# Segment copies ordered by token group: a linear-attention and expert-layer kernel on one core

## The chip, the cores and the metric

The kernel runs on one NeuronCore of one Trainium2 chip. The metric is the time of one execution on the device in microseconds. The core has five engines that run side by side: TensorE (PE in the rows; PEld is its weight load), VectorE (DVE), ScalarE (ACT), GpSimd (POOL) and SyncE (SP). Each has a sequencer that reads its instructions in order, and engines meet through semaphores. DMA transfers are issued from SP's and POOL's queues.

## What is computed

First a linear attention over q, k and v of shape (8, 8, 576, 64), then a layer of eight experts in which a hash of the token's id chooses the one expert of each token:

```python
q_s = exp(q - max(q)) / sum(...)          # over the head dimension
k_s = exp(k - max(k)) / sum(...)          # over the sequence
kv  = einsum('bhsd,bhse->bhde', k_s, v)
x   = einsum('bhsd,bhde->bhse', q_s, kv)  # regrouped as (4608, 512)
expert_idx = token_ids * 2654435761 % 8
for e in range(8):
    xe = x[expert_idx == e]
    out[expert_idx == e] = relu(xe @ w1[e]) @ w2[e]   # w1: 512 x 1024, w2: 1024 x 512
```

## The kernel before

The program is written engine by engine: every operation is appended to its engine's list in the order of the Python code, and `Emit._waits` adds the semaphore waits that its reads (R), writes (W) and partial writes (P) need. A write waits for an earlier write to the same buffer even on the same engine; only TensorE is excepted. Nothing reorders the lists.

**First stage, eight batches.** For batch b the loop of line 734 loads q, k and v (lines 493 to 497, from SP's queue), takes exponentials on ACT (lines 500 and 504, tiles eq and ek), transposes q on TensorE (line 514; the copies to qT are lines 524 to 529), casts v on DVE (line 509), forms kv (line 537) and its normalised form kvn (line 546), the row sums (lines 556 and 560), and attends (lines 564 and 569), which leaves the batch's tokens in xn. One batch later `sort` (lines 584 to 596) multiplies xn by one-hot matrices, so that the tokens of each of two groups (384 and 192 tokens) stand in order of expert, and ACT copies the result from PSUM to xs (line 595). There are two xs buffers, used in turn.

**Segments.** `segments` (lines 627 to 641) then copies, for each expert and each of the two groups, a window of fixed width (80 columns for group 0, 48 for group 1) out of xs into that expert's part of xT, at offsets that the data decide. The window is wider than the segment; what it writes too much is overwritten by the expert's next window, so the windows of one expert have to be written in order. The offsets are loaded into registers of the engine by `load_segments` (lines 612 to 625), one load for a batch. The buffers b_x5 and b_x7 have one entry per expert: the copy of group 1 of an expert waits for the copy of group 0 of the same expert. Each copy is preceded by a register instruction (line 636), which carries the waits. In batches 0 to 5 POOL does all 16 copies; in batches 6 and 7 DVE does experts 0 to 3 (8 copies a batch for DVE's half, of four experts) and POOL experts 4 to 7.

`segments` is a generator that yields once per expert, and `run` draws from it.

**Weights.** The weights go through POOL's queue. In the iteration of batch 6 the code issues four transfers for the two halves of w1 of expert 0 (`weights1_half`, line 661) in the midst of batch 5's copies. They wait for the load of k of batch 7 (the R of line 761), and their place in SBUF was that of q and k. In the iteration of batch 7 POOL issues w1 of expert 1 (line 653) and w2 of expert 0 (line 667), then loads registers and copies its half of batch 6.

**Second stage.** After the attention of batch 7, TensorE does two units of layer 1 of expert 0 (lines 790 and 791; line 676 is the matmul, a unit is eight of them, line 683 is ACT's ReLU), then the sort of batch 7 (line 588), and then the layers of all experts without another sort (lines 829 to 862; line 701 is layer 2).

Of the kernel before, what the change touches and what calls it, by code (L numbers as in the profile page):

```python
# [164 lines left out]
def fused_kernel(nc, q, k, v, moe_token_ids, moe_w1, moe_w2, out):  # L165
    B, H, S, DH = q.shape
    NTOK = moe_token_ids.shape[0]
    E, D, F = moe_w1.shape
# [324 lines left out]
    def load(b, p):  # L493
        for nm, dst, src, bb in (("d_q%d", qf, q, b_q), ("d_k%d", kf, k, b_k), ("d_v%d", vf, v, b_v)):
            em.dma("sync", nm % p, lambda e, dst=dst, src=src: e.dma_start(
                dst[p][:].rearrange("p h c d -> p h (c d)"),
                src[b].rearrange("(a h) (p c) d -> (h p) a (c d)", h=2, p=64)), W=[bb[p]])

    def exp_q(p, j):
        ac(lambda e: e.activation(eq[p][:, j, :, :, :].rearrange("p c a d -> p a c d"),  # L500
                                  qf[p][:, j::2, :, :], ACTF.Exp), R=[b_q[p]], W=[b_eq[p][j]])

    def exp_k(p):
        ac(lambda e: e.activation(ek[p][:].rearrange("p j c a d -> p a (j c) d"),  # L504
                                  kf[p][:].rearrange("p (a j) c d -> p a (j c) d", a=2), ACTF.Exp),
           R=[b_k[p]], W=[b_ek[p]])

    def cast_v(p):
        dv(lambda e: e.tensor_copy(out=vx[p][:, :, :, 0:DH], in_=vf[p][:]), R=[b_v[p]], W=[b_vx[p]])  # L509

    def transpose_q(p):

        def tr(e, j, c, o):
            return e.transpose(PBH[:, o:o + 128], eq[p][:, j, c, :, :].rearrange("p a d -> p (a d)"), ident[:])  # L514
        for j in range(2):
            em.op("pe", [lambda e, j=j, c=c: tr(e, j, c, 1024 * j + 128 * c) for c in range(8)],
                  R=[b_eq[p][j], bc["ident"]], W=[bk[j]])
        em.op("pe", [lambda e, j=j: tr(e, j, 8, 2048 + 128 * j) for j in range(2)], R=b_eq[p] + [bc["ident"]],
              W=[bk[2]])
        for j in range(2):  # L520
            o = qT[p][:, j, :, 0:512].rearrange("p h (c x) -> p h c x", x=64)
            i = PBH[:, 1024 * j:1024 * j + 1024].rearrange("p (c h x) -> p h c x", h=2, x=64)
            if j == 0:
                dv(lambda e, o=o, i=i: e.tensor_copy(out=o, in_=i), R=[bk[0]], W=[b_qT[p][0]])  # L524
            else:
                ac(lambda e, o=o, i=i: e.activation(o, i, ACTF.Copy), R=[bk[1]], W=[b_qT[p][1]])
        dv(lambda e: e.tensor_copy(out=qT[p][:, :, :, 512:576],
                                   in_=PBH[:, 2048:2304].rearrange("p (j h x) -> p j h x", h=2, x=64)),
           R=[bk[2]], W=[b_qT[p][2]])
# [25 lines left out]
    def qsum(p):  # L555
        em.op("pe", [lambda e, t=t, j=j, h2=h2: e.matmul(
            PB[:, 5, 8 * t + 4 * j + 2 * h2:8 * t + 4 * j + 2 * h2 + 2], qt(p, t, j, h2), pair1[:],
            start=True, stop=True) for t in range(T) for j in range(2) for h2 in range(2)],
            R=b_qT[p] + [bc["pair1"]], W=[bk[5]])
        dv(lambda e: e.reciprocal(out=rq[p][:].rearrange("p t g -> p (t g)"), in_=PB[:, 5, 0:8 * T]), R=[bk[5]],  # L560
           W=[b_rq[p]])
# [13 lines left out]
    def one_hot(b):  # L575
        p = b % 2
        for t in range(T):
            g, i = t // TG, t % TG
            dv(lambda e, g=g, i=i: e.tensor_scalar(  # L579
                out=oneh[p][g][:, i, :], in0=col16[:, 0:GW[g]], scalar1=pos[:, 2 * b + g, i:i + 1],  # L580
                scalar2=None, op0=ALU.is_equal),
               R=[b_pos, bc["col16"]], W=([b_oh[p][g]] if i == 0 else ()), P=(() if i == 0 else [b_oh[p][g]]))

    def sort(p, c0, bank):

        for g, bs in ((0, bk[bank:bank + 2]), (1, bk[bank + 2:bank + 3])):
            n = 3 - g
            em.op("pe", [lambda e, g=g, i=i, k=k, n=n: e.matmul(  # L588
                PB[:, bank + (k if g == 0 else 2), (0 if g == 0 else GW[1] * k):(GW[0] if g == 0 else GW[1] * (k + 1))],
                xn[p][:, 3 * g + i, 128 * (c0 + k):128 * (c0 + k) + 128], oneh[p][g][:, i, :],  # L590
                start=(i == 0), stop=(i == n - 1)) for k in range(2) for i in range(n)],
                R=b_xn[p][3 * g:3 * g + n] + [b_oh[p][g]], W=bs)
            src = PB[:, bank:bank + 2, 0:GW[0]] if g == 0 else \
                PB[:, bank + 2, 0:2 * GW[1]].rearrange("p (k x) -> p k x", k=2)
            ac(lambda e, g=g, src=src: e.activation(xs[p][:, c0:c0 + 2, XO[g]:XO[g] + GW[g]], src, ACTF.Copy),  # L595
               R=bs, P=b_xs[p][c0:c0 + 2])

    def fill(bank, n):

        em.op("pe", [lambda e: e.matmul(PB[:, bank, :], ident[:], ones[:, 0:1].to_broadcast([128, 512]),  # L600
                                        start=True, stop=True) for _ in range(n)],
              R=[bc["ident"], bc["ones"]], W=[bk[bank]])
# [23 lines left out]

    def segments(b, key="pool", half=None):
        p = b % 2
        for ee in range(E) if half is None else range(4 * half, 4 * half + 4):
            for g in range(2):  # L630
                def seg(e, ee=ee, g=g):
                    if half is None:
                        rs, o = regs[key, None, 0], 2 * E * g + 8 * (ee // 4) + ee % 4
                    else:
                        rs, o = regs[key, half, p], 8 * g + ee % 4
                    so = e.snap(rs[o], min_val=0, max_val=GW[g])  # L636
                    do = e.snap(rs[o + 4], min_val=CAPS * ee, max_val=CAPS * ee + CAP)
                    return e.tensor_copy(out=xT[:, :, bass.ds(do, SEG[g])],  # L638
                                         in_=xs[p][:, :, XO[g]:XO[g] + GW[g] + SEG[g]][:, :, bass.ds(so, SEG[g])])
                em.op(key, seg, R=b_xs[p] + ([] if b < B - 2 else [b_x5[ee]]), W=[(b_x5 if b < B - 2 else b_x7)[ee]])  # L640
            yield


    b_w1 = [[Buf(), Buf()] for _ in range(NW)]
# [13 lines left out]
    def weights1_half(ee, s, hf, R=()):  # L658
        fs = slice(hf * F // 2, hf * F // 2 + F // 2)
        for a in range(2):  # L660
            em.dma("pool", "d_w1h%d" % hf, lambda e, a=a: e.dma_start(
                w1b[s][64 * a:64 * a + 64, :, fs], moe_w1[ee].rearrange("(a g p) f -> a p g f", a=2, g=4)[a, :, :, fs]), R=R,
                W=([b_w1[s][hf]] if a == 0 else ()), P=(() if a == 0 else [b_w1[s][hf]]))
# [56 lines left out]
            R=[b_yo[y], b_idx], P=[b_out])  # L720


    def run(gen, n=E):
        for _ in range(n):
            if next(gen, 0) == 0:
                break
# [7 lines left out]
    for b in range(B):  # L734
        p = b % 2
        last = b == B - 1
        exp_k(p)
        transpose_q(p)
        if b > 0:
            if not last:  # L740
                fill(3, 2)
            sort(1 - p, 0, 3)
            if not last:
                fill(0, 2)
            sort(1 - p, 2, 0)
        cast_v(p)
        if b + 2 < B:
            load(b + 2, p)
        if not last:
            one_hot(b + 1)  # L750
            exp_q(1 - p, 0)
            exp_q(1 - p, 1)
        kv(p)
        qsum(p)
        if b == B - 2:
            for s, bs in enumerate(([b_q[0], b_k[0]], [b_v[0], b_q[1]])):
                b_w1[s], b_w2[s] = [Buf(*bs), Buf(*bs)], Buf(*bs)
            load_segments(b - 1, "pool")
            sg = segments(b - 1)
            run(sg, 4)  # L760
            weights1_half(0, 0, 0, R=[b_k[1]])
            weights1_half(0, 0, 1)
            run(sg)
        elif last:
            weights1(1, 1)
            weights2(0, 0)
            for x in (b - 1, b):
                load_segments(x, "pool", 1)
                load_segments(x, "dve", 0)
            run(segments(b - 1, "pool", 1))  # L770
        elif b > 0:
            load_segments(b - 1, "pool")
            run(segments(b - 1))
        fill(3, 2)
        attend(p, 0, 2, 3)
        attend(p, 2, 2, 6)
        attend(p, 4, 1, 5)
        if b == 0:
            segment_table()
            widths()  # L780
        if b == 1:
            overflow()
        if b == 2:
            load_widths()
# [197 lines left out]
```

## Time and profile before

| | us |
|---|---|
| median of 3 runs | 242.68 (242.46 to 242.97) |
| the profiled execution, its own time | 242.81 |
| its span, first to last instruction | 241.1 |
| TensorE busy with matmuls | 205.9 (85%) |
| POOL busy | 123.8 (51%) |
| POOL's 112 segment copies | 47.9 |
| DVE busy | 125.7 (52%) |
| ACT busy | 106.2 (44%) |

The profile shows one execution. The time is some 1.7 us longer than the span, and every step counted in the span is taken to count fully in the time. The shares are averages over two stages of unlike kind; what an edit is worth is read from the stretch where it acts and from what is waited for there.

### The profile page before, as it was taken

The numbers are of one execution on the slowest core, as the hardware profiler recorded it, in microseconds if no ns is written. First come the engines' busy times: TensorE is split into PE (matmuls) and PEld (weight loads), VectorE is DVE, ScalarE is ACT, GpSimd is POOL, SyncE is SP. The second block draws the span as 40 slices with busy tenths as digits, with TensorE's granted clock in tenths as the row PEclk, the third lists the DMA queues.
The fourth block names the chain that finished last, engine by engine and source line by source line (L and its number), as shares of the span: only waits on it lengthen the run. The fifth ranks groups of instructions, "written<-read, shape, count | busy, mean of one in ns | idle before, by whom it ended". The sixth has DMA issues, their size and how long they took to land.

```text
span 241.1 us, 4707 instructions
## 1 busy us (share of the span) xinstructions
PE 205.9 (85%) x1826; PEld 134.0 (56%) x1828; DVE 125.7 (52%) x273; ACT 106.2 (44%) x133; POOL 123.8 (51%) x227
## 2 busy tenths in 40 slices
PE   0459978999998533898999999999999999999991
PEld 0247746666766321475657475475584764855740
DVE  4868899899898353048995232242241322421320
ACT  2657679889769310365534133132141230321310
POOL 6500755757675678759000797661653715315143
PEclk9999999999999955599999999999999999999998
DMA  5999999999997009996999389999999899203123
GB/s 155 400 392 392 391 390 391 390 390 392 390 390 264 3 2 162 163 199 105 198 206 188 132 177 197 199 379 222 248 220 202 234 185 247 113 0 149 50 90 122
DMA packets 29775, 54.96 MB, mean 228 GB/s; under 512 B 2351, under 2 KB 11567, under 8 KB 29744
## 3 DMA queue, kind: packets, MB, share of 16 engines
q0 software_dynamic: 16544, 26.22, 52.2%
q1 hardware_dynamic: 13200, 28.35, 31.9%
q8 instruction: 16, 0.26, 0.4%
q14 instruction: 15, 0.12, 0.2%
HBM read 61.90 MB, written 10.49 MB: 300 GB/s over the span
## 4 chain that ended last, share of the span: by engine, by line
PE 65%; DVE 10%; POOL 8%; DMA 6%; issue 5%; POOLq 2%; ACT 1%; SPq 1%
PE ps L676 27%; PE ps L701 27%; POOL xT L638 6%; PE ps L588 6%; DMA vf<-in_v_dram 4%; DVE xn L569 4%; DVE oneh L579 2%; DMA w1b<-in_moe_w_dram 2%; PE ps L564 2%; PE ps L600 2%; POOL out_dram L717 2%; DVE kvn L546 1%; PE ps L537 1%; POOLq L636 1%; PE ps L811 1%
## 5 line engine op out<-in xcount | busy, mean ns | idle before, releaser
L717 POOL DMA_INDIRECT out_dram<-yo,idx x40 | 39.5, 988 | 71.5 <-ACT yo L711 31.9
L676 PE MATMUL ps<-xT,w1b 128*128 128x320 bf16 (+1 forms) x512 | 66.7, 291 | 9.3 <-DMA w1b<-in_moe_w_dram 7.6
L701 PE MATMUL ps<-w2b,hT 128*128 128x512 bf16 x320 | 70.4, 379 | 0.0
L676 PEld LDWEIGHTS ps<-xT,w1b 128*128 128x128 bf16 x512 | 50.4, 99 | 25.1 <-DMA w1b<-in_moe_w_dram 7.9
L638 POOL COPY xT<-xs x112 | 47.9, 452 | 25.4 <-POOL xT L638 12.0
L701 PEld LDWEIGHTS ps<-w2b,hT 128*128 128x128 bf16 x320 | 31.3, 98 | 36.3
L683 ACT ACTIVATE hT<-ps 128x640 bf16<-128x640 f32 x41 | 28.8, 703 | 48.8 <-PE ps L676 48.4
L711 ACT ACTIVATE yo<-ps 128x512 f32<-128x512 f32 x26 | 15.5, 597 | 54.1 <-PE ps L701 51.3
L685 DVE TENSOR_SCALAR hT<-ps 128x640 bf16<-128x640 f32 x23 | 19.0, 825 | 30.2 <-PE ps L676 30.2
L713 DVE COPY yo<-ps 128x512 f32<-128x512 f32 x14 | 9.7, 691 | 44.0 <-PE ps L701 40.3
L588 PE MATMUL ps<-oneh,xn 128*128 128x384 bf16 (+1 forms) x160 | 24.9, 307 | 2.0 <-DVE xn L569 1.0
L569 DVE TENSOR_TENSOR xn<-ps,rq 128x1024 bf16<-128x1024 f32 (+1 forms) x24 | 23.6, 1040 | 5.2 <-PE ps L564 5.2
L595 ACT ACTIVATE xs<-ps 128x768 bf16<-128x768 f32 (+1 forms) x32 | 18.7, 651 | 15.0 <-PE ps L588 8.9
L588 PEld LDWEIGHTS ps<-oneh,xn 128*128 128x128 bf16 x160 | 15.4, 102 | 13.5 <-DVE xn L569 3.6
L500 ACT ACTIVATE eq<-qf 128x1152 bf16<-128x1152 f32 x16 | 17.8, 1166 | 8.1 <-DMA qf<-in_q_dram 8.1
L504 ACT ACTIVATE ek<-kf 128x2304 bf16<-128x2304 f32 x8 | 17.0, 2128 | 3.2 <-DMA kf<-in_k_dram 3.1
L537 PE MATMUL ps<-vx,ek 64*128 64x130 bf16 x288 | 10.6, 228 | 4.0 <-DVE vx L509 4.0
L514 PE MATMUL ps<-ident,eq 128*128 128x128 bf16 x144 | 10.9, 231 | 3.5 <-ACT eq L500 2.5
L600 PE MATMUL ps<-ones,ident 128*128 128x512 bf16 x40 | 12.3, 391 | 1.5 <-DVE qT L524 1.5
L564 PEld LDWEIGHTS ps<-kvn,qT 128*128 128x128 bf16 x160 | 10.5, 107 | 4.5 <-DVE kvn L546 4.0
L564 PE MATMUL ps<-kvn,qT 128*128 128x128 bf16 x160 | 11.8, 236 | 0.9 <-DVE kvn L546 0.9
L667 POOL DMA_DIRECT2D w2b<-in_moe_w_dram x16 | 12.4, 801 | 0.1
(102 smaller groups left out, 147.6 us busy)
## 6 DMA issues: line engine op xcount, KB each, us to landing
qf<-in_q_dram SPq DMA_DIRECT2D x8, 1152.0 KB, 15.2
kf<-in_k_dram SPq DMA_DIRECT2D x8, 1152.0 KB, 15.5
vf<-in_v_dram SPq DMA_DIRECT2D x8, 1152.0 KB, 15.5
w2b<-in_moe_w_dram POOLq DMA_DIRECT2D x16, 512.0 KB
w1b<-in_moe_w_dram POOLq DMA_DIRECT2D x14, 512.0 KB, 9.3
w1b<-in_moe_w_dram POOLq DMA_DIRECT2D x4, 256.0 KB, 5.3
out_dram<-yo,idx POOLq DMA_INDIRECT x40, 3.5
tok<-in_moe_token_ids_dram SPq DMA_DIRECT2D x1, 36.0 KB, 2.7
```

The costliest lines, as they stand in the source:

```text
L500: ac(lambda e: e.activation(eq[p][:, j, :, :, :].rearrange("p c a d -> p a c d"), qf[p][:, j::2, :, :], ACTF.Exp), R=[b_q[p]], W=[b_eq[p][j]])
L564: em.op("pe", [lambda e, i=i, j=j, h2=h2: e.matmul(PB[:, bank + i, 256 * j + 128 * h2:256 * j + 128 * h2 + 128], qt(p, t0 + i, j, h2), kvn ...
L569: dv(lambda e: e.tensor_tensor(out=xn[p][:, t0:t0 + n, :].rearrange("p t (g x) -> p (t g) x", x=DH), in0=PB[:, bank:bank + n, :].rearrange ...
L588: em.op("pe", [lambda e, g=g, i=i, k=k, n=n: e.matmul(PB[:, bank + (k if g == 0 else 2), (0 if g == 0 else GW[1] * k):(GW[0] if g == 0 els ...
L595: ac(lambda e, g=g, src=src: e.activation(xs[p][:, c0:c0 + 2, XO[g]:XO[g] + GW[g]], src, ACTF.Copy), R=bs, P=b_xs[p][c0:c0 + 2])
L600: em.op("pe", [lambda e: e.matmul(PB[:, bank, :], ident[:], ones[:, 0:1].to_broadcast([128, 512]), start=True, stop=True) for _ in range(n ...
L638: return e.tensor_copy(out=xT[:, :, bass.ds(do, SEG[g])], in_=xs[p][:, :, XO[g]:XO[g] + GW[g] + SEG[g]][:, :, bass.ds(so, SEG[g])])
L676: em.op("pe", [lambda e, d=d, k=k: e.matmul(cut(PB[:, u + k, 0:H2]), w1b[s][:, d, 128 * (f + k):128 * (f + k) + 128], cut(rhs(d)), start=( ...
L683: ac(lambda e: e.activation(o, i, ACTF.Relu), R=bk[u:u + 2], W=[b_hT[hp][hf][f // 2]])
L685: dv(lambda e: e.tensor_scalar(out=o, in0=i, scalar1=0.0, scalar2=None, op0=ALU.max), R=bk[u:u + 2], W=[b_hT[hp][hf][f // 2]])
L701: em.op("pe", [lambda e, fc=fc: e.matmul(PB[:, u, :], hT[hp][:, fc, 128 * t:128 * t + 128], w2b[s][:, fc, :], start=(fc == 0), stop=(fc == ...
L717: em.dma("pool", "d_o%d" % y, lambda e: e.indirect_dma_start(out=out[:, :], out_offset=IndirectOffsetOnAxis(ap=idx[:, 5 * ee + t:5 * ee + ...
```

## The change

The two loops of `segments` change places, so that a batch's copies run over the eight experts for group 0 and then over the eight experts for group 1 (in the halves of batches 6 and 7, over four and four). The generator now yields after every copy, and `run` draws up to 16 by default. Where the first weights are issued, 8 copies of batch 5 are drawn ahead of them: 8 copies as before, but now all of group 0 rather than both groups of four experts.

```diff
     def segments(b, key="pool", half=None):
         p = b % 2
-        for ee in range(E) if half is None else range(4 * half, 4 * half + 4):
-            for g in range(2):
+        for g in range(2):
+            for ee in range(E) if half is None else range(4 * half, 4 * half + 4):
                 def seg(e, ee=ee, g=g):
...
                 em.op(key, seg, R=b_xs[p] + ([] if b < B - 2 else [b_x5[ee]]), W=[(b_x5 if b < B - 2 else b_x7)[ee]])
-            yield
+                yield
...
-    def run(gen, n=E):
+    def run(gen, n=2 * E):
...
             sg = segments(b - 1)
-            run(sg, 4)
+            run(sg, 8)
             weights1_half(0, 0, 0, R=[b_k[1]])
             weights1_half(0, 0, 1)
             run(sg)
```

On POOL, where batch 3 (xs_73) ends and batch 4 (xs_72) begins, with the load of the offsets (rgi) between them; ISA is the register instruction of a copy, the last two numbers of a copy are chunks and columns, and s_pool and s_act are the semaphores of POOL and ACT. Before:

```order
L636 ISA [waits s_pool]
L638 COPY xT<-xs_73 128x4x48
L636 ISA
L638 COPY xT<-xs_73 128x4x80
L636 ISA [waits s_pool]
L638 COPY xT<-xs_73 128x4x48
L621 TENSOR_LOAD rgi
L636 ISA [waits s_act]
L638 COPY xT<-xs_72 128x4x80
L636 ISA [waits s_pool]
L638 COPY xT<-xs_72 128x4x48
```

And now:

```order
L636 ISA [waits s_pool]
L638 COPY xT<-xs_73 128x4x48
L636 ISA [waits s_pool]
L638 COPY xT<-xs_73 128x4x48
L636 ISA [waits s_pool]
L638 COPY xT<-xs_73 128x4x48
L621 TENSOR_LOAD rgi
L636 ISA [waits s_act,s_pool]
L638 COPY xT<-xs_72 128x4x80
L636 ISA [waits s_pool]
L638 COPY xT<-xs_72 128x4x80
```

Every copy has a wait for POOL's own semaphore now, where every second one had it; its target is the copy eight places earlier and no longer the one just ahead.

On POOL around the first weights (w1b0, four transfers) in batch 5, with the semaphores of the loads of q and k (s_d_q0, s_d_k0, s_d_k1). Before:

```order
L638 COPY xT_49<-xs1_73 128x4x80
L636 ISA [waits s_pool]
L638 COPY xT_49<-xs1_73 128x4x48
L661 DMA w1b0_78<-in_moe_w1_dram 64x4x512 [waits s_d_k0,s_d_q0,s_d_k1]
L661 DMA w1b0_78<-in_moe_w1_dram 64x4x512 x3
L636 ISA
L638 COPY xT_49<-xs1_73 128x4x80
L636 ISA [waits s_pool]
L638 COPY xT_49<-xs1_73 128x4x48
```

And now:

```order
L638 COPY xT_49<-xs1_73 128x4x80
L636 ISA [waits s_pool]
L638 COPY xT_49<-xs1_73 128x4x80
L661 DMA w1b0_78<-in_moe_w1_dram 64x4x512 [waits s_d_k0,s_d_q0,s_d_k1]
L661 DMA w1b0_78<-in_moe_w1_dram 64x4x512 x3
L636 ISA [waits s_pool]
L638 COPY xT_49<-xs1_73 128x4x48
L636 ISA [waits s_pool]
L638 COPY xT_49<-xs1_73 128x4x48
```

The transfers keep their place as the ninth work of the batch and their waits; all eight copies of 80 columns are now ahead of them and all eight of 48 behind.

TensorE's, ACT's and SP's instructions keep their order. On DVE the 16 copies of batches 6 and 7 are reordered in the same way.

## Rows read from the trace of the kernel before

**Rows 1.** Chain of waits, 88 to 104 us: start, length, engine and line.

```profile
88.65 0.88 POOL w1b L661
89.53 4.68 DMA w1b<-in_moe_w_dram
94.26 2.33 PE ps L676 x8
...
99.68 4.10 PE ps L588 x20
103.79 6.53 PE ps L676 x48
```

**Rows 2.** A stretch: engines' busy us; then clock granted, DMA share, GB/s.

```profile
84.00:86.00 2.00, 2.00 (x38) 1.76 (x39) 0.41 (x1) 0.99 (x2) 1.20 (x3) 0.88 0.00 0
```

**Rows 3.** POOL in order of time: start, busy us, work; in brackets idle before, releaser.

```profile
73.48 0.46 POOL L638 COPY xT<-xs  x1 [1.88 <-ACT xs L595]
74.14 0.75 POOL L638 COPY xT<-xs  x2 [0.20 <-POOL xT L638]
...
78.23 1.92 POOL L638 COPY xT<-xs  x2 [0.20 <-POOL xT L638]
...
84.48 0.45 POOL L638 COPY xT<-xs  x1 [1.86 <-ACT xs L595]
...
88.65 2.76 POOL L661 DMA_DIRECT2D w1b<-in_moe_w_dram  x4 [0.32 <-issue]
```

**Rows 4.** Tile xT: POOL's copies (ns, first and last start); idle until (us, times).

```profile
L638 POOL COPY xT<-xs x112: 347/453/1654, 31.8 to 108.5; - x112
...
  POOL xT L638: 12.0, 56
```

**Rows 5.** Lines 621 and 624, register loads: count, ns min/median/max, first and last start.

```profile
L621 POOLq TENSOR_LOAD <-rgi x6: 2025/2033/2279, 29.3 to 82.3; - x6
...
L624 DVEq TENSOR_LOAD <-rgi x4: 597/598/846, 84.7 to 86.8; - x4
L624 POOLq TENSOR_LOAD <-rgi x4: 560/564/567, 96.8 to 98.6; - x4
```

**Rows 6.** ACT in order of time, 71 to 85 us.

```profile
71.69 2.28 ACT L595 ACTIVATE xs<-ps 128x768 bf16<-128x768 f32 x4 [2.37 <-POOL xT L638]
...
75.94 2.14 ACT L504 ACTIVATE ek<-kf 128x2304 bf16<-128x2304 f32 x1
...
82.71 2.28 ACT L595 ACTIVATE xs<-ps 128x768 bf16<-128x768 f32 x4 [3.72 <-POOL xT L638]
```

**Rows 7.** TensorE in order of time, 79 to 84 us.

```profile
79.14 1.47 PE L588 MATMUL ps<-oneh,xn 128*128 128x384 bf16 x10 [0.71 <-ACT qT L526]
...
83.96 0.65 PE L556 MATMUL ps<-pair,qT 128*128 128x2 bf16 x20 [2.22 <-ACT xs L595]
```

**Rows 8.** DVE in order of time, 78 to 91 us.

```profile
78.19 1.35 DVE L509 CAST vx<-vf 128x2304 bf16<-128x2304 f32 x1
...
82.00 0.88 DVE L546 TENSOR_TENSOR kvn<-ps,rk 64x256 bf16<-64x256 f32 x2
...
87.52 2.95 DVE L569 TENSOR_TENSOR xn<-ps,rq 128x1024 bf16<-128x1024 f32 x3 [2.46 <-PE ps L564]
```

**Rows 9.** POOL in order of time, weight issues of batch 7 and after.

```profile
96.77 1.53 POOL L667 DMA_DIRECT2D w2b<-in_moe_w_dram  x2
...
110.39 1.27 POOL L653 DMA_DIRECT2D w1b<-in_moe_w_dram  x2
```

**Rows 10.** Load of k of batch 7: issue on SP; KB and us to landing.

```profile
59.46 2.81 SPq L495 DMA_DIRECT2D kf<-in_k_dram  x1
...
kf<-in_k_dram SPq DMA_DIRECT2D x1, 1152.0 KB, 15.6
```

**Rows 11.** Line 653, the two issues at 95.6 and 96.2 (w1 of expert 1).

```profile
L653 POOL DMA_DIRECT2D w1b<-in_moe_w_dram x2: 610/614/617, 95.6 to 96.2; - x2
...
DMA to landing us min/median/max: 5.7/6.6/7.6
```

## The prediction, made before the changed kernel ran

> **What bounds the kernel now.** I read the chain of waits first, from the last instruction backwards. From 104 us to the end it is TensorE almost without a break. The loose part lies before that: TensorE starts the expert layers at 94.26 us, released by the first half of expert 0's w1, whose second DMA is issued at 89.53 and lands 4.68 later; the first is issued at 88.65 [rows 1]. Just before, from 84 to 86, the DMA engines move nothing [rows 2]: memory waits for POOL's issue.
>
> POOL's instructions in order of time show why [rows 3]. The four w1 issues stand behind the first eight segment copies of batch 5. A first copy (80 columns) takes 0.45 us; then pairs follow, a 48-column copy and the next expert's 80-column copy, 0.75 long with 0.20 idle ahead, released by POOL itself. That idle is the second copy of an expert waiting for the first, one instruction earlier, because both write the same expert's buffer; there are 56 such waits on POOL, 12.0 us [rows 4]. Between batches there is another hole, 1.88 us: the load of the offsets into registers takes 2.03 [rows 5] and starts with the last copy of a batch. So a batch costs POOL 11.0 us (73.48 to 84.48). POOL is behind, and ACT with it: the evictions into xs wait for POOL to have read the buffer, 2.37 and 3.72 us [rows 6], and the latter holds TensorE for 2.22 [rows 7].
>
> **The change, part by part.** No instruction goes or comes; 112 copies on POOL and 16 on DVE change order. The two copies of an expert are now eight apart (four in the halves), so the wait is there but its target is done.
>
> *A POOL batch.* Before, 16 copies need about 8 x (0.75 + 0.20) = 7.6 us. Without the idle, 8 x 0.75 = 6.0. Single copies of 0.45 and 0.35 sum to 0.80 where a pair takes 0.75, so neighbours overlap by 0.05 and more joints are now of that kind: 5.6 to 6.0. One copy pair per batch stretches, 1.92 for 0.75, beside DVE's cast of v (78.19 to 79.54) [rows 3, 8]; I keep these 1.2 us.
>
> *Does a satisfied wait cost nothing?* The nearest row is the w1 issue at 110.39. It waits for DVE and for two earlier transfers, waits that were met, and the row shows no idle ahead of it [rows 9]: they were passed while the engine worked on the w2 pair before it. I take nothing; the bound above is 0.20 a copy, the slower rival below.
>
> *Does the register load hide?* A load for batch 6 started at 96.8 [rows 5], while the w2 pair that stands ahead of it ran from 96.77 to 98.30 [rows 9]: the sequencer passes queued work. Before, the wait at the last copy forbade that. Now the last wait is for the eighth copy of the batch, done about 3.3 us after the start, and 2.03 later is 5.4, inside the 5.6 to 6.0. So I let the hole vanish; the bound is the whole 1.88.
> [...]
> [...]
>
> So a batch costs 5.6 + 1.2 = 6.8 us if the load hides, and 6.0 + 1.2 + 1.9 = 9.1 at most if not. From batch 0's first copy at 31.8 [rows 4], five batches end at 65.8 or at 77.3. The data of batch 5 is there at 72.0 (next part). So with hidden loads POOL drops from the chain; without them it stays on it.
>
> *What is late next, ACT.* Without its 2.37 wait the eviction of batch 5 ends at about 72.0 instead of 74.0. The exponential of k for batch 7 started at 75.94 [rows 6]; its data is issued at 59.46 and lands 15.6 later, at 75.06 [rows 10]. The load allows 0.85 and no more. The sort of batch 6 (79.14, released by ACT [rows 7]), then kv and kvn (82.00 + 0.88 = 82.88 [rows 8]) come 0.85 earlier: kvn ends at 82.03. The 3.72 wait goes too, so the row sums (83.96 [rows 7]) follow kv at 80.9 and no longer delay attention, which runs from 82.05 to about 83.4 (20 matmuls, 1.3 at full clock).
>
> *The weights.* With xs full at 72.0, eight 80-column copies need 8 x 0.40 to 0.45 = 3.2 to 3.6 and the issue follows after 0.3: 75.6 to 75.9. Its wait for k of batch 7 (75.06) is met. From first issue to landing was 94.21 - 88.65 = 5.56 [rows 1], so 81.2 to 81.5, up to 1 us more while v of batch 7 still arrives. That is before TensorE is free, at 83.4. The second copies of expert 0, now behind the four issues (2.76 [rows 3]), are done near 79.3 and nobody waits for them.
>
> *TensorE from there.* The first two layer-1 units started at 94.26 and the sort of batch 7 at 99.68 [rows 1], at a granted clock of 0.50, which fell within 84 to 86 us [rows 2] after the 2.22 idle. At full clock a unit is 6.53 / 6 = 1.09, with ACT's 0.8 between (5.42 from start to sort, less two units of 2.33): 83.4 + 3.0 = 86.4. The sort then waits for xn of batch 7. Before, xn started at 87.52 [rows 8], after four register loads on DVE from 84.7 to 87.4 [rows 5] behind the row sums' reciprocal. That reciprocal now follows kvn, the loads end about 85.2, and after two of xn's three instructions the sort starts at 87.4. Two sorts of ten at 1.4 (1.47 with the drain [rows 7]) end at 90.2; they ended at 103.79. That is 13.6 earlier, of which 2.7 is clock (see the first rival).
>
> *After that* TensorE has the same work. The next thing that could be late is w1 of expert 1: its second DMA, issued at 96.17 (95.57 + 0.60), landed 7.6 later [rows 11], 15.1 after the first w1 issue. From 75.8 this is 90.9; needed at 90.2 + 2.2 = 92.4. Later weights are issued after batch 7's copies, which follow the sort and get shorter. DVE's 16 copies lose waits of the same kind, and TensorE has six units (6.5 us) to do after the sort before it needs their first result. The shift lasts to the end. Against the profiled execution, 242.81 us: 242.8 - 13.6 = 229.2; I add 0.1 for v sharing memory with the weights: **229.3 us**. The median of the three runs shown is 0.13 under the profiled one, inside the rounding.
>
> **Rivals.**
> *The clock falls all the same.* TensorE pauses 0.8 and 1.0 us between 84.5 and 87.4. For it: the clock fell after 2.2 idle; against: no pause here is that long. Two units with their pause in 5.4 (94.26 to 99.68) and a sort of 4.10 [rows 1] end at 83.4 + 9.5 = 92.9, 10.9 earlier: 231.9.
>
> *POOL still binds.* If the loads stay open and neighbours overlap no more than now, batch 5 starts at 77.3, the issue comes near 80.6 and w1 lands at 86.1. At full clock the sort ends at 86.1 + 5.8 = 91.9, but expert 1's w1 (80.6 + 15.1 = 95.7) then stops TensorE at 94.1; that point was 103.79 + 2.2 = 106.0, so 10.3 earlier: 232.5. At half clock, after 2.7 idle, 95.6: 234.6.
>
> *Each wait costs its 0.20 even when met*: the slower one. All 16 copies would carry the gap: 16 x 0.20 + 8 x 0.80 = 9.6 a batch instead of 7.6, 10 us over five batches, and 8 x 0.65 = 5.2 instead of 3.85 (0.45 + 0.20 + 0.35 + 3 x 0.95) for the eight ahead of the issue. The issue would come at 100 and all of it lasts: about 254. It decides as soon as POOL's sequencer holds copies back until the one before has ended. Against it are the issues that pass met waits [rows 9].
>
> *The order does nothing*: if the weights were held by something else than POOL's queue. No row has it: k lands 13 us before the issue.
>
> **How the numbers follow.** The forecast (228.3 to 230.3) 0.5; clock falls 0.22; POOL binds 0.20; a smaller gain, to 242, 0.03; no change 0.01; slower 0.04. To hold eight in ten the range takes the clock and POOL cases: 228.2 to 234.6. A change under 0.2% (0.5 us) can't be told from none here: faster 0.95, same 0.01, slower 0.04.
>
> **What would show it.** Idle of POOL released by POOL's own copies near zero instead of 12.0; a batch of copies in 6 to 7 us; register loads that begin while copies of the old batch still run; no eviction waiting for POOL; the first w1 issue at 75 to 76; layer 1 released by TensorE's own order near 83.4; the sort of batch 7 released by xn; a full clock throughout. It is wrong if gaps of 0.2 stand ahead of copies, if layer 1 still starts on a DMA, or if a later weight stops TensorE for the gained time.

## The result

| | before | after |
|---|---|---|
| median | 242.78 us (242.46 to 242.97, 4 runs) | 228.98 us (228.21 to 229.22, 4 runs) |
| ratio | | 0.9427, 95% interval 0.9402 to 0.9452 |
| the profiled execution | 242.81 us | 228.91 us |
| its span | 241.1 us | 227.1 us |

The forecast was 229.3, its range 228.2 to 234.6. The kernel is 5.7% faster.

POOL after the change, in order of time; columns as in [rows 3]:

```profile
31.33 13.43 POOL L638 COPY xT<-xs  x32 [2.28 <-issue]
45.91 5.50 POOL L638 COPY xT<-xs  x16 [1.15 <-ACT xs L595]
...
63.15 5.51 POOL L638 COPY xT<-xs  x16 [3.13 <-ACT xs L595]
71.78 3.20 POOL L638 COPY xT<-xs  x8 [3.12 <-ACT xs L595]
75.17 2.77 POOL L661 DMA_DIRECT2D w1b<-in_moe_w_dram  x4 [0.19 <-issue]
77.92 3.45 POOL L638 COPY xT<-xs  x8
81.32 1.23 POOL L653 DMA_DIRECT2D w1b<-in_moe_w_dram  x2
```

Batches 0 and 1 are one row of 32 copies with no idle between them: the 0.20 ahead of every pair and the 1.88 hole between batches are both gone. The copies of a later batch take 5.50 us where a batch took 11.0 with its gaps, its hole and the pair beside the cast, and now POOL waits for ACT's data (3.12), not ACT for POOL. The first weight issue is at 75.17 instead of 88.65 [rows 3].

Tile xT after, columns as in [rows 4]:

```profile
L638 POOL COPY xT<-xs x112: 337/446/1577, 31.3 to 93.0; - x112
...
  ACT xs L595: 14.2, 5
```

Lines 621, 624 and 653 after, columns as in [rows 5, 11]; the last are the two issues of expert 1's w1:

```profile
L621 POOLq TENSOR_LOAD <-rgi x6: 2027/2037/2262, 28.8 to 66.6; - x6
...
L624 DVEq TENSOR_LOAD <-rgi x4: 597/598/842, 81.3 to 83.5; - x4
...
L653 POOL DMA_DIRECT2D w1b<-in_moe_w_dram x2: 615/624/632, 81.3 to 81.9; - x2
...
DMA to landing us min/median/max: 7.1/8.0/9.0
```

The row "POOL xT L638: 12.0, 56" of [rows 4] has no answer: no copy waits for POOL any more. The last load of line 621 starts at 66.6, in the midst of the batch that runs from 63.15 to 68.66.

DVE and TensorE after, in order of time, columns as in [rows 7, 8]:

```profile
81.84 0.41 DVE L560 RECIPROCAL rq<-ps 128x40 f32<-128x40 f32 x1
84.17 2.95 DVE L569 TENSOR_TENSOR xn<-ps,rq 128x1024 bf16<-128x1024 f32 x3 [1.92 <-PE ps L564]
```

```profile
81.87 1.29 PE L564 MATMUL ps<-kvn,qT 128*128 128x128 bf16 x20 [0.15 <-DVE kvn L546]
83.00 1.25 PE L676 MATMUL ps<-xT,w1b 128*128 128x320 bf16 x8
85.04 1.26 PE L676 MATMUL ps<-xT,w1b 128*128 128x320 bf16 x8 [0.80 <-ACT hT L683]
86.58 2.78 PE L588 MATMUL ps<-oneh,xn 128*128 128x384 bf16 x20 [0.28 <-DVE xn L569]
89.20 6.68 PE L676 MATMUL ps<-xT,w1b 128*128 128x320 bf16 x48
96.77 3.47 PE L676 MATMUL ps<-xT,w1b 128*128 128x0 bf16 x25 [0.88 <-DVE cs L438]
```

The counterpart of the row at 89.20 in the same view of before:

```profile
103.62 6.68 PE L676 MATMUL ps<-xT,w1b 128*128 128x320 bf16 x48
```

Layer 1 starts at 83.00 with no bracket: the weights are there. The row at 89.20 is 14.4 us earlier than its counterpart (103.79 in the chain of [rows 1]). Every later step stays 14.4 earlier, down to the issue of the last store (222.91, before 237.34). The same window as in [rows 2], after:

```profile
84.00:86.00 2.00, 1.20 (x9) 0.70 (x8) 1.83 (x2) 0.70 (x1) 2.00 (x7) 1.00 1.08 196
```

The granted clock is 1.00 where it was 0.88 on its way to 0.50 (86 to 102 us), and the DMA engines, which moved nothing, work all the time.

### The profile page after: what moved, and what is told of

The parts are those of the page before. It is cut to its first block, busy times and chain, and to the rows that moved or that the text cites. A ratio compares the mean times of both kernels' runs of the same rounds, so it can differ in the third digit from the quotient of the medians.

```text
span 227.1 us, 4693 instructions
## 1 busy us (share of the span) xinstructions
PE 199.1 (88%) x1804; PEld 130.9 (58%) x1828; DVE 123.8 (55%) x273; ACT 106.6 (47%) x133; POOL 118.0 (52%) x227
## 4 chain that ended last, share of the span: by engine, by line
PE 63%; DVE 12%; DMA 12%; issue 4%; POOL 3%; ACT 2%; SPq 2%; POOLq 1%; DVEq 0%; ACTq 0%
PE ps L701 29%; PE ps L676 24%; DMA kf<-in_k_dram 7%; DMA vf<-in_v_dram 5%; DVE xn L569 4%; PE ps L588 4%; PE ps L537 2%; SPq L495 2%; POOL xT L638 2%; PE ps L564 1%; DVE vx L509 1%; DVE kvn L546 1%; ACT eq L500 1%; PE ps L600 1%; DVE zz L436 1%
## 5 line engine op out<-in xcount | busy, mean ns | idle before, releaser
L701 PE MATMUL ps<-w2b,hT 128*128 128x512 bf16 x312 | 68.6, 379 | 0.4
L676 PE MATMUL ps<-xT,w1b 128*128 128x320 bf16 (+1 forms) x512 | 64.6, 286 | 1.7 <-DVE cs L438 0.9
L676 PEld LDWEIGHTS ps<-xT,w1b 128*128 128x128 bf16 x512 | 49.7, 98 | 16.1 <-DVE cs L438 1.2
L638 POOL COPY xT<-xs x112 | 42.1, 433 | 16.6 <-ACT xs L595 14.2
L588 PE MATMUL ps<-oneh,xn 128*128 128x384 bf16 (+1 forms) x160 | 23.4, 295 | 3.3 <-DVE xn L569 2.8
L588 PEld LDWEIGHTS ps<-oneh,xn 128*128 128x128 bf16 x160 | 14.4, 97 | 14.4 <-DVE xn L569 5.7
L537 PEld LDWEIGHTS ps<-vx,ek 64*128 64x128 bf16 x288 | 9.2, 99 | 5.4 <-issue 5.2
L564 PEld LDWEIGHTS ps<-kvn,qT 128*128 128x128 bf16 x160 | 9.3, 99 | 5.2 <-DVE kvn L546 5.1
L600 PE MATMUL ps<-ones,ident 128*128 128x512 bf16 x26 | 9.2, 390 | 3.3 <-DVE qT L527 2.3
```

Source lines behind the costliest of these rows:

```text
L537: fns.append(lambda e, j=j, c=c, h2=h2, r=r: e.matmul(PB[:, 6 + h2, 130 * j:130 * j + 130], ek[p][r, j, c, :, :].rearrange("p a d -> p (a ...
L588: em.op("pe", [lambda e, g=g, i=i, k=k, n=n: e.matmul(PB[:, bank + (k if g == 0 else 2), (0 if g == 0 else GW[1] * k):(GW[0] if g == 0 els ...
L638: return e.tensor_copy(out=xT[:, :, bass.ds(do, SEG[g])], in_=xs[p][:, :, XO[g]:XO[g] + GW[g] + SEG[g]][:, :, bass.ds(so, SEG[g])])
L676: em.op("pe", [lambda e, d=d, k=k: e.matmul(cut(PB[:, u + k, 0:H2]), w1b[s][:, d, 128 * (f + k):128 * (f + k) + 128], cut(rhs(d)), start=( ...
L701: em.op("pe", [lambda e, fc=fc: e.matmul(PB[:, u, :], hT[hp][:, fc, 128 * t:128 * t + 128], w2b[s][:, fc, :], start=(fc == 0), stop=(fc == ...
```

## The experiments

The theory: POOL's pace through batches 0 to 5 decides, because the weights stand behind its copies; the pace was lost to waits for the copy just ahead, twice, as gaps of 0.20 and as a register load that can't run ahead. Rivals: the place of the first weights alone; the clock alone; the number of waits rather than their distance.

**Which batches make the gain?** In the first run only batches 0 to 4 have the new order (its edit is shown), in the second only batch 5 (`b == B - 3` in place of `b < B - 3`).

```diff
-        for g in range(2):
-            for ee in range(E) if half is None else range(4 * half, 4 * half + 4):
+        es = list(range(E) if half is None else range(4 * half, 4 * half + 4))
+        for g, ee in [(g, ee) for g in range(2) for ee in es] if b < B - 3 else [(g, ee) for ee in es for g in range(2)]:
+            if True:
```

> New order of the copies in batches 0 to 4 only; batches 5, 6 and 7 keep the old order (four experts, then the first weights, then four experts). If the gain comes from POOL's pace over the first five batches, batch 5 still starts at 71.8, the first weights' issue comes at 71.8 + 3.85 + 0.3 = 75.9 instead of 75.2, expert 1's w1 some 0.8 to 1.5 us later than with the whole change (needed at 91.4, landed at 90.9), and the time is 229.2 to 230.3 us, nearly the whole gain. If the order around the weights in batch 5 makes the gain, the time stays above 238.

Measured: 229.47 us, ratio 0.9467 (0.9437 to 0.9498).

> The complement: the new order in batch 5 alone, the old one in all other batches. By the theory of POOL's pace batch 5 starts at 84.5 as before, the issue comes some 0.5 us earlier, expert 1's w1 perhaps 1 us earlier, and the time is 241.5 to 242.7 us. If the order around the weights makes the gain, the time is under 235.

Measured: 240.98 us, ratio 0.9943 (0.9917 to 0.9970), half a microsecond under what was expected. So nearly the whole gain is the pace of the five batches ahead. Most of the half microsecond that the first run lacks shows in TensorE's rows, the stretch after the sort of batch 7:

```profile
89.81 2.34 PE L677 MATMUL ps<-xT,w1b 128*128 128x320 bf16 x16
92.46 4.52 PE L677 MATMUL ps<-xT,w1b 128*128 128x320 bf16 x32 [0.32 <-DMA w1b<-in_moe_w_dram]
```

With the old order around the weights, w1 of expert 1 is issued at 84.26 and TensorE waits for it, as expected.

**Is it the distance of the wait?** Three runs keep the new order and bring one half of the old loss back. First, a wait for the copy just ahead on every copy of batches 0 to 5:

```diff
+    b_chain = Buf()
...
-                em.op(key, seg, R=b_xs[p] + ([] if b < B - 2 else [b_x5[ee]]), W=[(b_x5 if b < B - 2 else b_x7)[ee]])
+                em.op(key, seg, R=b_xs[p] + ([] if b < B - 2 else [b_x5[ee]]), W=[(b_x5 if b < B - 2 else b_x7)[ee]] + ([b_chain] if half is None else []))
```

> The new order, but in batches 0 to 5 each copy on POOL also waits for the copy just ahead of it (one more buffer that all of them write). This prices the rival in which all 16 copies of a batch carry the gap: 16 x 0.20 + 8 x 0.80 = 9.6 us a batch and the hole of 1.88 between batches back, so 11.5 us a batch against 11.0 before (the copy beside DVE's cast left out), the first issue near 91 to 100 and a time of 245 to 254 us. If the gap hangs on the kind of pair and not on waiting for the copy just ahead, the time stays near 229 to 235.

Measured: 253.06 us, ratio 1.0436 (1.0400 to 1.0471). The tile xT in this run, idle of POOL (us, times):

```profile
  POOL xT L640: 17.9, 89
```

That is 0.20 a time, and the same order of copies is now slower than the kernel before. So a wait for the copy just ahead cost 0.20 here whatever the pair was, and a met wait nothing: after the change all 16 copies of a batch have one and stand in one row without idle. The rival of the prediction that priced this case (254) was a right price for a case that didn't come.

Second, the register load made to wait for the last copy of the batch before, which leaves the gaps closed and opens the hole:

```diff
-        em.raw(key, ld, R=[b_rg])
+        em.raw(key, ld, R=[b_rg] + (b_x5 if half is None else []))
```

> The new order, but the register load of a batch waits until the last copy of the batch before it is done. Theory (the hidden load is worth about 2 us a batch on POOL, of which most is absorbed because batches then come no faster than the loads): a batch in 7.8 us, first weights issued near 78.9, layer 1 waits again for w1 by 1 to 2 us and expert 1's w1 by up to 2.6: 230.5 to 231.7. Rival (only the gaps between copies mattered): 229.0.

Measured: 234.94 us, ratio 0.9674 (0.9642 to 0.9706). Third, pairs of experts, so that a wait's target is two copies back:

```diff
-        for g in range(2):
-            for ee in range(E) if half is None else range(4 * half, 4 * half + 4):
+        es = list(range(E)) if half is None else list(range(4 * half, 4 * half + 4))
+        for k in range(0, len(es), 2):
+            for g, ee in ((0, es[k]), (0, es[k + 1]), (1, es[k]), (1, es[k + 1])):
```

> The copies in pairs of experts: group 0 of two experts, then group 1 of the same two, so that a waited-for copy stands two places back, not one and not eight; 8 copies (four experts) stay ahead of the weights. Theory (any distance over one removes the 0.20 us, but the register load then starts only with the last two copies and is mostly open): no idle between copies, a batch in about 7.4 us, first weights issued near 77.4, 229.0 to 229.8. Rival (the distance has to cover more of the queue for the gap to go): gaps of 0.1 to 0.2 us stay, weights issued at 80 or later, 231.5 or more.

Measured: 233.85 us, ratio 0.9615 (0.9555 to 0.9674). Two copies apart is enough for the gap (0.2 us of such idle in all), but not for the load, which stands behind a wait for the last copy but two: the hole stays. POOL in the run with pairs:

```profile
74.83 2.78 POOL L639 COPY xT<-xs  x8 [1.79 <-ACT eq L500]
77.91 3.47 POOL L662 DMA_DIRECT2D w1b<-in_moe_w_dram  x4 [0.29 <-issue]
```

In both runs POOL has no gaps and a hole, and both are 5 to 6 us slower than the whole change. Both expectations were 3 to 5 us too low; the time of the run with pairs lies in its rival's range, but the rival's sign, gaps between copies, isn't there. POOL and TensorE of the second run, in order of time:

```profile
68.28 6.73 POOL L638 COPY xT<-xs  x16 [2.29 <-ACT ek L504]
77.27 4.33 POOL L638 COPY xT<-xs  x8 [2.27 <-ACT ek L504]
81.55 2.76 POOL L661 DMA_DIRECT2D w1b<-in_moe_w_dram  x4
```

```profile
87.23 2.32 PE L676 MATMUL ps<-xT,w1b 128*128 128x320 bf16 x8 [3.34 <-DMA w1b<-in_moe_w_dram]
90.34 2.31 PE L676 MATMUL ps<-xT,w1b 128*128 128x320 bf16 x8 [0.80 <-ACT hT L683]
92.45 4.65 PE L588 MATMUL ps<-oneh,xn 128*128 128x384 bf16 x20
```

Two things that I hadn't counted stand there. Eight copies beside DVE's cast of v (78.73 to 80.11) take 4.33 instead of 3.20; and the pause of 3.34 is followed by units of 2.32 and a sort of 4.65, at a granted clock of 0.50 (88 to 96 us; 1.25 and 2.78 at 1.00 in the run of the change). Here a late issue cost its lateness and then the clock. That is the second rival of the prediction with its half clock (234.6).

**What does the cast do to an issue?** In the run with pairs the issues fell on the cast, and the second transfer took 8.14 to land. To price this by itself, the new order with the four issues behind all 16 copies of batch 5, and then the same with the cast of batch 7 on ACT:

```diff
-            run(sg, 8)
+            run(sg)
             weights1_half(0, 0, 0, R=[b_k[1]])
```

```diff
-        cast_v(p)
+        if last:
+            ac(lambda e: e.activation(vx[p][:, :, :, 0:DH], vf[p][:], ACTF.Copy), R=[b_v[p]], W=[b_vx[p]])
+        else:
+            cast_v(p)
```

> The new order, but the first weights' four issues stand behind all 16 copies of batch 5. The issue then starts near 77.4 and falls on DVE's cast of v (77.8 to 79.1). If that only moves the issue by 2.2 us, the second transfer lands at 83.2 to 83.5, TensorE waits 0.3 us, expert 1's w1 comes at its old time, and the time is 229.0 to 229.6. If a cast on DVE holds up what POOL issues, as the run with pairs of experts suggests, the issues are stretched, no data flows until the cast is over, the weights land near 86 to 87, TensorE idles 3 us and works at half clock for some 6 us, and the time is 232 to 234.5.

Measured: 230.57 us, ratio 0.9504 (0.9470 to 0.9537).

> The run with the first weights behind all of batch 5's copies, with the cast of v of batch 7 on ACT instead of DVE. One look at the issues, which again start near 77.9. If DVE's cast stretched them, none takes over 0.9 us now (one took 1.94), the four take 2.8 us instead of 3.8, the DMA engines move weights between 79 and 80, and the second transfer lands 4.7 to 5.6 after its issue. If the order on POOL's queue did it, one still takes 1.9 us. The time is not the question: ACT's 2.1 us for the cast delay kv, attention and the sort by up to 3 us (230 to 233).

Measured: 231.32 us, one execution. Line 661 with the cast on DVE (ns, first and last start; us to landing), and two windows of the same run (columns as in [rows 2]):

```profile
L661 POOL DMA_DIRECT2D w1b<-in_moe_w_dram x4: 631/648/1935, 77.9 to 81.1; - x4
...
DMA to landing us min/median/max: 5.6/6.6/7.8
```

```profile
78.00:80.00 2.00, 1.53 (x12) 0.87 (x10) 1.37 (x2) 1.77 (x4) 2.00 (x2) 1.00 0.04 8
80.00:82.00 2.00, 1.92 (x59) 1.65 (x58) 0.66 (x3) 0.98 (x2) 2.00 (x4) 1.00 0.59 69
```

The same with the cast on ACT:

```profile
L661 POOL DMA_DIRECT2D w1b<-in_moe_w_dram x4: 628/646/882, 77.8 to 80.0; - x4
...
DMA to landing us min/median/max: 4.4/5.6/7.0
```

```profile
78.00:80.00 2.00, 1.60 (x12) 0.88 (x10) 0.00 (x0) 1.76 (x4) 2.00 (x4) 1.00 0.19 24
80.00:82.00 2.00, 0.00 (x0) 0.00 (x0) 0.00 (x0) 2.00 (x3) 2.00 (x4) 1.00 1.06 160
```

The issues start at the same time; without DVE's cast beside them the longest takes 0.88 us instead of 1.94, and from 80 to 82 us the DMA engines move 160 GB/s instead of 69. So it is DVE's cast (1.36 us) that holds POOL's issues, for 1.1 us in all (3.83 against 2.77). By what the cast holds them, no run here shows. POOL's copies beside a cast are longer by as much (4.33 for 3.20); there the cast wasn't moved to see. The cast can be the one that is longer: beside the same four issues, in the run with batches 0 to 4 alone, it took 1.85.

The time of the first run lies between the two expectations: the mechanism is the second's, but TensorE waited only 1.74 us and its clock stayed at 1.00. Nor does the length of a pause alone decide on the clock. In the run with the cast on ACT TensorE stood idle for 2.97 us, longer than the 2.22 before the change, and worked on at a clock of 1.00 (82 to 84 us). The first row is of the run with the cast on DVE, the others of that with the cast on ACT:

```profile
85.45 1.26 PE L676 MATMUL ps<-xT,w1b 128*128 128x320 bf16 x8 [1.74 <-DMA w1b<-in_moe_w_dram]
```

```profile
82.71 1.21 PE L537 MATMUL ps<-vx,ek 64*128 64x130 bf16 x36 [2.97 <-ACT vx L747]
86.24 1.25 PE L676 MATMUL ps<-xT,w1b 128*128 128x320 bf16 x8
```

**The first weights alone, and the clock alone.** Both from the kernel before. One issues the first weights ahead of the register load and of all of batch 5's copies; the other puts 24 matmuls, whose result nobody uses, ahead of the first layer-1 unit, so that TensorE doesn't stand idle:

```diff
-            load_segments(b - 1, "pool")
-            sg = segments(b - 1)
-            run(sg, 4)
             weights1_half(0, 0, 0, R=[b_k[1]])
             weights1_half(0, 0, 1)
-            run(sg)
+            load_segments(b - 1, "pool")
+            run(segments(b - 1))
```

```diff
     run(segments(B - 2, "dve", 0))
+    fill(0, 24)
```

> The old order, with the four w1 issues ahead of batch 5's register load and copies. Theory (what is lost is POOL's lateness, and moving the issues past one batch's copies buys just those 5.8 us): first issue near 82.7, landing near 88.3, layer 1 starts there instead of at 94.26: 236.5 to 237.5. Rival (the position of the weights alone, not POOL's pace, is the whole gain): 229 to 231.

Measured: 242.98 us, ratio 1.0001 (0.9966 to 1.0036).

> The old order of copies, and 24 matmuls of 128x512 (no use is made of their result) on TensorE between the attention of batch 7 and the first layer-1 unit, where it stood idle for 7.6 us at the lower clock. Theory (the clock is a part of its own, worth 2.7 us of the 13.9): w1 still lands near 94.2, the two units and the sort then run at full clock and end 2.3 to 2.7 us earlier, 240.1 to 240.5. Rival (all of the gain is the time at which the weights come, the clock made up elsewhere): 242.8 as before.

Measured: 242.73 us, ratio 1.0001 (0.9975 to 1.0027). Two misses of one kind. TensorE, first weights ahead:

```profile
94.40 3.58 PE L588 MATMUL ps<-oneh,xn 128*128 128x384 bf16 x20
97.82 2.34 PE L676 MATMUL ps<-xT,w1b 128*128 128x320 bf16 x16
104.17 7.20 PE L676 MATMUL ps<-xT,w1b 128*128 128x320 bf16 x32 [4.02 <-DMA w1b<-in_moe_w_dram]
```

TensorE, with the 24 matmuls:

```profile
97.64 2.77 PE L588 MATMUL ps<-oneh,xn 128*128 128x384 bf16 x20
100.25 2.34 PE L676 MATMUL ps<-xT,w1b 128*128 128x320 bf16 x16
104.64 6.19 PE L676 MATMUL ps<-xT,w1b 128*128 128x320 bf16 x32 [2.05 <-DMA w1b<-in_moe_w_dram]
```

Both are ahead after the sort (97.82 and 100.25; before 103.62), and both then wait for w1 of expert 1, which stands behind all of batch 5's copies on POOL. The rest goes with the clock, which is low again behind that wait (0.50 with the first weights ahead, 0.61 with the 24 matmuls, means of 104 to 108 us): the 32 matmuls take 7.20 and 6.19 us where they took 4.52 in the row at 92.46 above. With the first weights ahead, 4.02 of wait and 2.68 of clock are more than the 5.80 that were gained; with the 24 matmuls, 2.05 and 1.67 are more than the 3.37. Neither the place of the first weights nor the clock was worth anything by itself.

The next run issues that weight early too; beside the first weights ahead of the copies it has

```diff
             weights1_half(0, 0, 1)
+            weights1(1, 1)
             load_segments(b - 1, "pool")
...
         elif last:
-            weights1(1, 1)
```

> The kernel before with the old order of copies, and both the first weights and w1 of expert 1 issued ahead of all of batch 5's copies. In the run that moved the first weights alone, TensorE waited 4.0 us for w1 of expert 1, where the gain went. If that weight alone took the gain, it is now there by 95 to 96, no wait stands before it, and the time is 236.5 to 238.0 us. If POOL's copies themselves bind (the segments of batches 5 to 7 come another 1.3 us later), the time stays at 240 to 243.

Measured: 240.78 us (238.97 to 242.72), ratio 0.9920 (0.9883 to 0.9957), the second of the two cases. In the profiled execution (239.23, one of the faster ones) TensorE is 8.0 us ahead after the sort (95.67 against 103.62), with no wait for w1 of expert 1. DVE and TensorE show where half of that went:

```profile
104.33 0.37 DVE L433 TENSOR_TENSOR zz<-gsum,sx 128x128 f32<-128x128 f32 x1 [3.77 <-POOL xT L638]
```

```profile
124.56 2.85 PE L809 MATMUL ps<-selB,selA 128*128 128x80 bf16 x40 [2.81 <-DVE selA L480]
```

DVE's work for the table of output rows (some 20 us of it) starts when POOL's last copies are done (104.3; 108.8 before), and TensorE needs the table. It waits 2.81, and the table's matmuls take 2.85 where they take 1.60 in the run of the change, at a clock of 1.00: 4.1 of the 8.0, and this execution is 3.6 faster than that of before. In the run of the change the same row of DVE stands at 93.55 and TensorE has no such wait. POOL's pace thus held three things, one behind the other: the first weights, expert 1's weight, and the table.

**A faster version.** Three edits on what is late after the change, beside a second run of the change itself on the same chip. `half_unit(k, bank)` is half of the second layer-1 unit, four matmuls into one bank and their ReLU on ACT:

```diff
         cast_v(p)
+        if last:
+            for x in (b - 1, b):
+                load_segments(x, "dve", 0)
...
             weights1_half(0, 0, 1)
+            weights1(1, 1)
             run(sg)
         elif last:
-            weights1(1, 1)
...
-                load_segments(x, "dve", 0)
...
-    for f in range(0, FC // 2, 2):
-        l1(0, f, 0, 0, True)
+    l1(0, 0, 0, 0, True)
+    half_unit(0, 2)
+    half_unit(1, 0)
...
-        l1(ee, f, 0, (6, 3, 0)[i % 3], True)
+        l1(ee, f, 0, (6, 3, 0, 6, 0, 3)[i], True)
```

> The changed kernel itself again, as the neighbour of the next run on the same chip: 228.9 us (228.2 to 229.3).

Measured: 228.60 us, ratio 0.9431 (0.9394 to 0.9467).

> The change and three edits on what is late next. DVE's four register loads for batches 6 and 7 stand right behind the cast of v of batch 7 instead of behind the row sums' reciprocal, so xn of batch 7 starts near 82.7 instead of 84.2; the second layer-1 unit is done in two halves, the first in bank 2, so that TensorE has 0.55 us of work in its 0.80 pause: the sort starts at 85.6 to 85.9 instead of 86.58, 0.7 to 0.9 earlier. w1 of expert 1 is issued ahead of the 48-column copies of batch 5, so that it isn't due before that. The third: the six units after the sort end in banks 0 then 3 rather than 3 then 0, which takes away the 0.88 pause before the unit behind them, if that pause is the wait for ACT to free bank 0. Together 1.5 to 1.8 us: 227.1 to 227.5. If the pause of 0.88 is DVE's copies instead, 228.0 to 228.3; if the register loads don't hold xn back, 228.0 to 228.4.

Measured: 226.66 us (226.32 to 226.84), ratio 0.9340 (0.9305 to 0.9375), 1.9 us below its neighbour. TensorE:

```profile
84.52 0.71 PE L794 MATMUL ps<-xT,w1b 128*128 128x320 bf16 x4
85.48 0.72 PE L794 MATMUL ps<-xT,w1b 128*128 128x320 bf16 x4 [0.25 <-ACT hT L683]
86.03 2.77 PE L588 MATMUL ps<-oneh,xn 128*128 128x384 bf16 x20
88.64 12.58 PE L676 MATMUL ps<-xT,w1b 128*128 128x320 bf16 x96
```

In its neighbour the sort starts at 87.11 and the last row at 89.73: 1.1 us came ahead of the sort, and the pause of 0.89 after the first 48 matmuls is gone, so it was the wait for a bank that ACT had just been given to read, though the profile names a DVE line as its end; that line ends at 96.11 in this run, and TensorE passes the place near 95.3 (88.64 + 6.68). The time is 0.4 under the range that was expected. How the 1.1 divides between the register loads and the split unit wasn't tried.

## Why the prediction was right

*POOL.* The gaps and the hole went as worked out, and that is most of the gain. A batch takes 5.5, just under the 5.6 to 6.0. The 1.2 beside DVE's cast, which I added to each batch, falls away where POOL has caught up, since its copies then end before the cast begins (68.66 and 68.88); only in batch 5 one copy of 48 columns is still beside it (1.42 us, in the 3.45 at 77.92). Batches 0 and 1 do carry it (13.43 for 32 copies, 6.7 a batch). It cost nothing either way: POOL waits for data from batch 2 on.

*The register load.* This was the step with the widest bounds: the rows of before had shown a load pass one issue queued behind one at work, and that it would pass the last eight copies of a batch was my estimate. The row at 66.6 settles it: when the load began, one copy was 0.1 us from its end (66.66) and seven, 0.29 us apart, were still to start; the last ended at 68.66. Whether it could have passed more, no run here shows.

*ACT and the first weights.* xs of batch 5 was full at 71.5 (72.0 worked out), the issue came at 75.17 (75.6 to 75.9): the copies took 3.20, the low end. Layer 1 started at 83.00, by TensorE's own order, as forecast (83.4). The 0.1 us that the sum adds for v was an estimate, and no run shows it as a cost in time: while v landed (77.8), the first two weight transfers took 4.7 and 5.1 us to land where they took 4.3 and 4.7 before, but TensorE waited for neither.

*The sort of batch 7* is the mis-sized term: forecast to start at 87.4, it started at 86.58, and it ended 14.4 earlier instead of 13.6. I let DVE's four register loads begin behind the row sums' reciprocal. They began at 81.3, before it ran (81.84): the sequencer had passed the reciprocal, whose wait was met, while DVE was still at kvn. It is what I had counted on for POOL and did not apply to DVE. xn so started at 84.17 instead of 85.2.

*The end.* Of the 14.4 the time shows 13.9: in the profiled execution the span ends 3.2 us after the last store's issue (222.91 + 0.96 to 227.1), where it was 2.8 before (237.34 + 0.96 to 241.1). The second run of the change had 2.5, so this is scatter. A sort that came 0.8 earlier than in the sum and an end that came 0.4 later partly cancel, which is luck: 229.3 against 228.9.

*Expert 1's w1* landed at 90.9 (81.9 + 9.0), to the tenth as forecast, but by luck: the first weights' issue was 0.6 earlier than in the sum, and from there to this landing it took 15.7 us, not 15.1 (the second transfer 9.0 instead of 7.6). It was due at 91.5 (89.20 + 2.34) rather than 92.4: the margin was 0.6 us, not 1.5. The run with the old order around the weights used it up. The table of output rows isn't in the prediction at all. It was ready near 113.4, 1.7 us before TensorE came to it (115.12), so nothing was lost there; in the run with all weights ahead of the copies it was what bound.

*The clock.* It stayed at 1.00 up to 220 us, so the first rival didn't come. But the sum names 2.7 of the gain as clock, as if it were a part by itself. The run with the 24 matmuls shows that it isn't: with the clock at 1.00 through the sort and POOL late, the next weight took it back. The second rival was sized well for the run whose load waits for the last copy: batch 5 at 77.27 where 77.3 was worked out, and 234.94 us against 234.6. The run with pairs (233.85) has its hole too, but its issue came at 77.91, before the 80.6 of the sum, and the four issues then took 3.47 beside the cast where they took 2.77 after the change.

## What to carry to other kernels

Where POOL waited for its own last instruction, both the gap (0.20 us a time) and what its sequencer couldn't do ahead (a register load of 2 us a batch) were lost here; order independent pieces so that the target of each wait lies several instructions back, and far enough for what is to run ahead. Before crediting a gain to one late transfer, look down the same queue for the next one: here moving the first weight, or keeping the clock up, gave nothing until the whole queue was faster. Where it can be arranged, a queue that issues transfers shouldn't issue them beside a long cast on DVE: it cost 1.1 us of POOL's time here.

## What the runs showed of the hardware

- A wait on POOL for the copy just ahead cost 0.20 us a time in one run (17.9 for 89; 0.19 to 0.21 on 64 of the 66 occasions up to 86 us, 0.49 and 0.58 on the others); waits for one two places back cost 0.2 us in all, and for one eight back none showed. Before the change DVE's own copies had gaps of 0.19 of the same kind.
- A load into registers passed one copy at work on POOL and seven behind it; on DVE it passed an operation whose wait was met. Where a wait for a recent copy stood in the way, 1.8 to 2.3 us of hole stayed (0.9 to 1.0 where the last copy itself was stretched to 1.2 or 1.3).
- DVE's cast of 128 x 2304 (1.36 us) stretched one of POOL's issues from 0.88 at most to 1.94; in the 2 us behind it the DMA engines moved 69 GB/s, and 160 with the cast on ACT.
- After pauses of 0.80, 1.74 and, in one run, 2.97 us TensorE's granted clock stayed at 1.00, and a unit took 1.25 us. Around or behind pauses of 2.22 [rows 2, 7], 3.17, 3.34 and 4.02 it fell to 0.50, where a unit took 2.3; around one of 2.05 its mean was 0.61 over 4 us. So the length of the pause alone didn't decide, and no run here shows what does.
